# One stream of tokens in blocks of 256, 8 x 512 and 256 for the first part of a fused attention, convolution and Fourier kernel

## The chip, the core and the metric

The kernel runs on one core of a Trainium2 chip. TensorE (PE in the profile, with its weight loads as PEld) multiplies a moving tile by a stationary tile of 128x128 into PSUM, where the kernel keeps eight tiles of up to 512 fp32 columns (called banks here). VectorE (DVE) and ScalarE (ACT) do the elementwise work and read PSUM, GpSimd (POOL) does a few small copies, and SyncE (SP) issues the DMAs. The engines run their own lists of instructions in order and wait for each other through semaphores. The metric is the device time of one execution in microseconds (us). The kernel before takes 1354.01 us, the median of three runs (1353.06 to 1356.51).

## The reference

Three stages follow each other on 8 batches of 576 tokens and 512 features. All arithmetic is fp32.

```python
# 1. attention inside chunks of 64 tokens, 8 heads of 64 features
scores = scale * q_c @ k_c.T ; attn = softmax(scores) ; x = attn @ v_c      # x: 8 x 576 x 512
# 2. a gated layer with a 3-tap convolution over a batch's tokens
h = np.maximum(x @ w_in, 0.0)                                               # 512 -> 1024
conv_out = sum(conv_w[k] * hp[:, k:k + S, :] for k in range(3))             # hp: h with a zero token at both ends
x = h * sigmoid(conv_out) @ w_out                                           # 1024 -> 512
# 3. Fourier mixing over tokens and features, normalisation, and a wide layer
u = x + real(fft(fft(x, axis=1), axis=2)) ; un = (u - mu) / sqrt(var + 1e-6)
y = u + np.maximum(un @ w_ch1, 0.0) @ w_ch2                                 # 512 -> 2048 -> 512
```

## The kernel before

**Precision.** A product that has to be as good as fp32 is made of three fp32r matmuls: each operand is split into a high part (an fp32r copy, ACT) and a low part (the fp32 value minus the copy, DVE), and high x high, high x low and low x high are added in PSUM. Helper `split` (L279) records the two halves: `L280` is the ACT copy, `L281` the DVE subtraction.

**First part (about 0 to 600 us), the one that the change is about.** Tokens lie in the free dimension. Each batch is cut into 256 and 320 tokens (`NTOK`, L23), so there are 16 pieces, numbered i. For each piece:

- `attention(i, q)` (L364) does four heads at a time (q = 0, 1): scores (PE L386), maximum, exponential and normalisation (DVE L392 to L403, ACT L398), transposes of the attention (PE L411, ACT L414), values (PE L429 and L433), and the split of the result into tiles `x0..` (ACT L442, DVE L443). A piece of 320 tokens has five chunks, of which the fifth has instructions of its own. The `x0` tiles exist twice, once for pieces of either length.
- `m_step(i, f)` (L448), eight times: the product with one 128-wide slice of `w_in` (12 matmuls, PE L466), ReLU (ACT L486 or L496), the three taps (ACT L490 or L497, DVE L483 twice), the gate (ACT tanh L501, DVE L503), and the split into `gh` and `gl`. The last three tokens of h of the first piece of a batch are kept by POOL (L489) and put before those of the second piece (L495).
- `x_step(i, f)` (L514), eight times: the product of `gh`, `gl` with a slice of `w_out` into four PSUM banks, one per 128 features (12 matmuls, PE L534). After the eighth, ACT empties the four banks into `xlo` (tokens 0 to 287, with a mirrored copy of 32 tokens) and `xhi` (the other half in reverse), L550 to L572. The next piece's first x_step needs those banks empty.

Piece 0 uses plain fp32 matmuls (L457, L528) on weights that are still being turned from 64-bit words into fp32 (`to_float32`, DVE L293 to L297); only when a weight slice has been used there is it split.

After every second piece a batch is complete: `fold` (L577) adds and subtracts its halves, `d_step` (PE L642), `s_step` (PE L675) and `u_step` (PE L697) do the Fourier sums, and u goes to DRAM. `fold` makes `g` tiles on DVE, POOL repeats 33 columns of them twice (L594), and 355 columns are split. `fold_last` does that for the last batch in halves. `weight_sums` prepares `w_ch1` on DVE and PE-free time in between.

**Second part (about 610 us to the end).** `group` (PE L909) and `second` (PE L976) do the wide layer. Nothing in it is changed.

**What sets the order.** Every operation is recorded with an engine, an estimated cost, a priority `prio` and its dependencies. `Plan.emit` (L153) then writes one list per engine: at each step it takes the engine that can start first, and on it the ready operation with the least `prio`. Buffers are rings: `buf(pool, tag, n, ...)` waits for the n-th buffer before it. PSUM has two rings of four banks: tag `x` (the x_step's accumulators) and tag `o` (everything else). Priorities of the first part count in steps of one m_step; an x_step stands `lag` = 2.5 steps behind its m_step.

Of the kernel before, what the change touches and what calls it, by code (L numbers as in the profile page):

```python
# [8 lines left out]
F32 = mybir.dt.float32  # L9
# [9 lines left out]
B = 8  # L19
# [3 lines left out]
NTOK = (256, 320)  # L23
NOUT = (256, 322)
# [200 lines left out]
def kernel(  # L225
    ctx: ExitStack,
    tc: tile.TileContext,
    qk_a: bass.AP,
    qk_b: bass.AP,
    v_a: bass.AP,  # L230
    v_b: bass.AP,
# [15 lines left out]
    NH = 2 * B  # L247
# [66 lines left out]
    def load_dft(prio):  # L314
# [16 lines left out]
        h = buf("d", "fg", 2, [128, 640], F32R)  # L331
# [10 lines left out]
    early += [("d", tag, 1 + (tag == "fg")) for tag in ("f00", "f10", "f01", "f11", "fg")]  # L342
    early += [("s", "ds0", 1), ("s", "ds1", 1), ("s", "xlo", 2), ("s", "xhi", 1), ("d", "dd0", 1), ("d", "dd1", 1), ("d", "fw", 1)]
# [20 lines left out]
    def attention(i, q, prio):  # L364
        b, c = divmod(i, 2)
        n = NTOK[c] // 64
        hps = (2 * q, 2 * q + 1)
        qk, v = [], []
        for p, hp in enumerate(hps):
            qk.append(buf(*(("s", "xlo", 2) if (i, hp) == (0, HP - 1) else ("a", "qk", 3)), [128, 2, NTOK[c]]))  # L370
            load(qk[p], lambda hp=hp: (qk_a, qk_b)[c][b, hp], 1024 * NTOK[c], prio - 12 + p)
        for p, hp in enumerate(hps):
            v.append(buf("a", "v", 6, [128, NTOK[c]]))
            load(v[p], lambda hp=hp: (v_a, v_b)[c][b, hp], 512 * NTOK[c], prio - 10 + p)

        s = [buf("ps", "o" if i else "x", 4, [128, n, 64]) for _ in range(2)]
        low, high = slice(0, 64), slice(64, 128)
        half = (low, high)

        def qk_unit():  # L380
            todo = [(h, p, 2 * j + u, 2 * p + j, u) for j in range(2) for p in range(2) for u in range(2) for h in range(2)]
            if n == 5:
                todo += [(h, p, 4, 4, p) for p in range(2) for h in range(2)]
            for h, p, k, slot, u in todo:
                t, ks = qk[p](), slice(64 * k, 64 * k + 64)
                pe.matmul(s[h]()[half[u], slot, :], t[half[h], 0, ks], t[half[h], 1, ks], start=True, stop=True)  # L386
# [8 lines left out]
        for h in range(2):  # L395
            def exp(h=h):
                for k in range(n):
                    act.activation(out=es()[:, at_es(h, k), :], in_=s[h]()[:, k, :], func=ACT.Exp, scale=0.125, bias=mx()[:, h, k:k + 1], accum_out=sm()[:, at_es(h, k), :])  # L398

            op("ACT", 291 * n, exp, prio, r=[s[h], mx], w=[es, sm])  # L400
# [5 lines left out]
        tps = [buf("ps", "o", 4, [128, 4, 128])] + ([buf("ps", "o", 4, [128, 1, 128])] if n == 5 else [])  # L406

        def tr_unit():
            flat = es().rearrange("p a k -> p (a k)")
            for k in range(n):  # L410
                pe.transpose(tps[k // 4]()[:, k % 4, :], flat[:, 128 * k:128 * k + 128], ident)  # L411

        op("PE", 109 * n, tr_unit, prio + 2, r=[es], w=tps, spare=1)
        aop(512, lambda: act.copy(out=at()[:, 0:4, :], in_=tps[0]()), prio + 2, [tps[0]], [at], True)  # L414
        if n == 5:
            aop(128, lambda: act.copy(out=at()[:, 4:5, :], in_=tps[1]()), prio + 2, [tps[1]], [at], True)

        xp = [buf("ps", "o", 4, [128, 2, 2, 64]) for _ in range(2)] + ([buf("ps", "o", 4, [128, 2, 1, 64])] if n == 5 else [])
        hl = [buf("a", f"x0{k}{c}{q}", 1, [128, 2, n, 64], F32R if i else F32) for k in range(2 if i else 1)]
        for p, hp in enumerate(hps):  # L420
            x0[i, hp] = [Part(t, p) for t in hl]

        def pv_unit():
            for p in range(2):
                for u in range(2):
                    us = half[u]
                    for h in range(2):
                        for j in range(2):
                            pe.matmul(xp[j]()[half[h], p, u, :], v[p]()[half[j], 128 * u + 64 * h:128 * u + 64 * h + 64], at()[half[j], 2 * h + p, us], start=True, stop=True)  # L429
            if n == 5:  # L430
                for p in range(2):
                    for h in range(2):
                        pe.matmul(xp[2]()[half[h], p, 0, :], v[p]()[half[h], 256:320], at()[half[h], 4, half[p]], start=True, stop=True)  # L433

        op("PE", 210 + 142 * n, pv_unit, prio + 4, r=[*v, at], w=xp, after=[o for t in hl if t.before for o in t.before.readers])
        for j, x in enumerate(xp):
            part = lambda t, j=j: t()[:, :, 2 * j:min(2 * j + 2, n), :]
            k = 256 if j < 2 else 128
            if not i:
                aop(k, lambda x=x, part=part: act.copy(out=part(hl[0]), in_=x()), prio + 4, [x], [hl[0]], True)  # L440
                continue
            aop(k, lambda x=x, part=part: act.copy(out=part(hl[0]), in_=x()), prio + 4, [x], [hl[0]], True)  # L442
            vop(k, lambda x=x, part=part: dve.tensor_tensor(part(hl[1]), x(), part(hl[0]).bitcast(F32), op=ALU.subtract), prio + 4, [x, hl[0]], [hl[1]])  # L443
# [3 lines left out]

    def m_step(i, f, prio):  # L448
        c = i % 2
        n, no = NTOK[c], NOUT[c]  # L450
# [31 lines left out]
        def conv(k, lo, hi, src):  # L482
            vop(hi - lo, lambda: dve.scalar_tensor_tensor(cv()[:, lo:hi], in0=h()[:, src:src + hi - lo], scalar=tap(k), in1=cv()[:, lo:hi], op0=ALU.mult, op1=ALU.add), prio, [h, cw, cv], [cv], scalars=1)  # L483

        if c == 0:
            aop(256, lambda: act.activation(out=h()[:, :256], in_=acc(), func=ACT.Relu), prio, [acc], [h], True)  # L486
            hs[f] = buf("a", "hs", 9, [128, 3])
            keep = hs[f]
            op("POOL", 130, lambda: pool.tensor_copy(out=keep(), in_=h()[:, 253:256]), prio, r=[h], w=[keep])  # L489
            aop(256, lambda: act.activation(out=cv()[:, :256], in_=h()[:, :256], func=ACT.Copy, scale=tap(1)), prio, [h, cw], [cv], scalars=1)  # L490
            conv(0, 1, 256, 0)
            conv(2, 0, 255, 1)
        else:
            keep = hs[f]
            op("POOL", 130, lambda: pool.tensor_copy(out=h()[:, :3], in_=keep()), prio, r=[keep], w=[h])  # L495
            aop(320, lambda: act.activation(out=h()[:, 3:323], in_=acc(), func=ACT.Relu), prio, [acc], [h], True)  # L496
            aop(322, lambda: act.activation(out=cv()[:, :322], in_=h()[:, 1:323], func=ACT.Copy, scale=tap(1)), prio, [h, cw], [cv], scalars=1)  # L497
            conv(0, 0, 322, 0)
            conv(2, 0, 321, 2)
# [3 lines left out]
        vop(no, lambda: dve.scalar_tensor_tensor(to(), in0=cv()[:, :no], scalar=1.0, in1=h()[:, c:c + no], op0=ALU.add, op1=ALU.mult), prio, [cv, h], [cv if i else gh])  # L503
# [10 lines left out]
    def x_step(i, f, prio):  # L514
        b, c = divmod(i, 2)
        no = NOUT[c]
# [19 lines left out]
        if i < NH - 1 or f < FT - 4:  # L536
# [661 lines left out]
```

## Time and profile before

| | |
|---|---|
| median of three runs | 1354.01 us |
| profiled execution, its own time | 1353.37 us |
| its span (first to last instruction) | 1351.6 us |
| PE busy over the span | 1316.9 us (97%), 11040 matmuls |
| DVE, ACT, POOL busy | 1047.6 us (78%), 799.9 us (59%), 78.3 us (6%) |
| chain that ended last, by engine | PE 84%, DVE 9%, ACT 4% |
| mean granted TensorE clock | 0.994 of 2.4 GHz |

The 1.8 us between span and time lie outside the first and the last instruction. A matmul's busy time in a row is its latency, and matmuls overlap: the distance from one start to the next, or the length of a run of matmuls in the chain divided by their number, is what one costs in a stream. In the same way an ACT or DVE instruction's record overlaps the next one's.

### The profile page before, as it was taken

The page shows a single profiled execution, that of the slowest core. Times are in us where ns is not written, and L with a number is a line of the kernel's source. Part 1 is how long each engine was busy: PE and PEld are TensorE (multiplying, and loading weights), DVE is VectorE, ACT ScalarE, POOL GpSimd, SP SyncE. Part 2 cuts the span into 40 slices and gives each one's busy share as a digit, 9 for nine tenths or more (in the row PEclk, how much of TensorE's full clock was granted, in tenths as well). Part 3 has the DMA queues.
Part 4 walks back from the last instruction along what each step waited for, and adds up shares of the span by engine and source line. Part 5 has one row for each costly group of instructions (what it writes and reads, how often), then busy time and mean ns, then how long its engine had stood idle before and what let it go on. Part 6 is the DMA issues. An engine that isn't in the chain of part 4 may idle for free.

```text
span 1351.6 us, 28891 instructions
## 1 busy us (share of the span) xinstructions
PE 1316.9 (97%) x11040; PEld 1247.4 (92%) x11040; DVE 1047.6 (78%) x2028; ACT 799.9 (59%) x2132; POOL 78.3 (6%) x195
## 2 busy tenths in 40 slices
PE   5899999999999999998999999999999999999999
PEld 4799999999999999997999888888899999999998
DVE  7999888878987676867877858665498777777773
ACT  6777677867676776655765656566653333333331
POOL 1111020102010010210000000000000000000000
PEclk9999999999999999998999999999999999999999
DMA  8533525331632132136865766778755554554441
GB/s 309 151 93 116 169 66 178 99 121 53 191 110 80 53 117 73 51 107 201 251 206 173 222 199 182 231 218 264 212 157 177 161 172 140 158 172 134 164 141 40
DMA packets 154059, 206.46 MB, mean 153 GB/s; under 512 B 11072, under 2 KB 102848, under 8 KB 153920
## 3 DMA queue, kind: packets, MB, share of 16 engines
q1 hardware_dynamic: 153920, 204.61, 48.5%
q8 instruction: 87, 1.43, 0.4%
q14 instruction: 52, 0.43, 0.1%
HBM read 130.51 MB, written 74.06 MB: 151 GB/s over the span
## 4 chain that ended last, share of the span: by engine, by line
PE 84%; DVE 9%; ACT 4%; issue 1%; POOL 0%; DVEq 0%; ACTq 0%; POOLq 0%
PE x L909 22%; PE x L976 15%; PE o L976 12%; PE x L534 11%; PE o L466 11%; PE o L909 4%; PE o L642 2%; PE o L675 2%; ACT es L398 1%; DVE cv L483 1%; PE o L697 1%; PE o L808 1%; PE o L429 1%; PE o L386 1%; PE o L411 1%
## 5 line engine op out<-in xcount | busy, mean ns | idle before, releaser
L280 ACT CAST sxh<-raw 128x1024 fp32r<-128x1024 f32 (+1 forms) x143 | 146.0, 1029 | 193.5 <-PE o L976 84.2
L466 PE MATMUL o<-x,wih 128*128 128x320 f32 (+1 forms) x960 | 200.4, 302 | 2.6 <-DVE u L702 1.2
L281 DVE TENSOR_TENSOR sxl<-raw,sxh 128x1024 fp32r<-128x1024 f32 (+1 forms) x143 | 169.6, 1194 | 26.2 <-ACT sxh L280 26.1
L909 PE MATMUL x<-sxh,th 128*128 128x512 f32 (+1 forms) x480 | 177.5, 370 | 1.1 <-ACT sum L893 0.6
L909 PE MATMUL x<-sxh,tl 128*128 128x512 f32 (+1 forms) x480 | 176.4, 368 | 0.0
L909 PE MATMUL x<-sxl,th 128*128 128x512 f32 (+1 forms) x480 | 176.3, 367 | 0.0
L976 PE MATMUL x<-tl,sxh 128*128 128x256 f32 x576 | 163.0, 283 | 0.0
L976 PE MATMUL x<-th,sxl 128*128 128x256 f32 x576 | 163.0, 283 | 0.0
L976 PE MATMUL x<-th,sxh 128*128 128x256 f32 x576 | 163.0, 283 | 0.0
L466 PEld LDWEIGHTS o<-x,wih 128*128 128x128 f32 x960 | 153.0, 188 | 5.8 <-DVE x L443 2.0
L483 DVE SCALAR_TENSOR_TENSOR cv<-h,cw,cv 128x255 f32<-128x255 f32 (+2 forms) x256 | 128.9, 513 | 23.7 <-ACT cv L497 15.5
L534 PE MATMUL x<-gh,woh 128*128 128x322 f32 (+1 forms) x480 | 145.1, 302 | 0.0
L534 PE MATMUL x<-gl,woh 128*128 128x322 f32 (+1 forms) x480 | 142.5, 297 | 0.6 <-DVE gl L281 0.6
L534 PE MATMUL x<-gh,wol 128*128 128x322 f32 (+1 forms) x480 | 142.2, 296 | 0.0
L466 PE MATMUL o<-x,wil 128*128 128x320 f32 (+1 forms) x480 | 142.2, 296 | 0.1
L976 PE MATMUL o<-th,sxh 128*128 128x256 f32 x432 | 122.3, 283 | 0.0
L976 PE MATMUL o<-tl,sxh 128*128 128x256 f32 x432 | 122.3, 283 | 0.0
L976 PE MATMUL o<-th,sxl 128*128 128x256 f32 x432 | 122.3, 283 | 0.0
L976 PEld LDWEIGHTS x<-th,sxh 128*128 128x128 f32 x576 | 110.6, 192 | 0.2
L976 PEld LDWEIGHTS x<-tl,sxh 128*128 128x128 f32 x576 | 110.6, 192 | 0.0
L976 PEld LDWEIGHTS x<-th,sxl 128*128 128x128 f32 x576 | 110.6, 192 | 0.0
L885 DVE TENSOR_TENSOR u<-x,u 128x256 f32<-128x256 f32 (+2 forms) x112 | 55.8, 499 | 67.6 <-PE x L976 39.3
(287 smaller groups left out, 3166.8 us busy)
## 6 DMA issues: line engine op xcount, KB each, us to landing
raw<-h_scr SPq DMA_DIRECT2D x72, 512.0 KB, 5.2
h_scr<-sum SPq DMA_DIRECT2D x72, 256.0 KB, 3.1
u<-u_scr SPq DMA_DIRECT2D x66, 256.0 KB, 3.3
qk<-in_qk_b SPq DMA_DIRECT2D x32, 320.0 KB, 3.4
h_scr<-sum SPq DMA_DIRECT2D x48, 192.0 KB, 2.7
out_y<-u SPq DMA_DIRECT2D x35, 256.0 KB, 2.5
wide<-in_w_ch SPq DMA_DIRECT2D x16, 512.0 KB, 4.9
u_scr<-u SPq DMA_DIRECT2D x32, 256.0 KB, 2.6
```

Of the source, the lines that this page charges most:

```text
L280: aop(n, lambda: act.copy(out=cut(h()), in_=cut(src())), prio, [src], [h], psum, after=after)
L281: vop(n, lambda: dve.tensor_tensor(cut(l()), cut(src()), cut(h()).bitcast(F32), op=ALU.subtract), prio, [src, h], [l])
L386: pe.matmul(s[h]()[half[u], slot, :], t[half[h], 0, ks], t[half[h], 1, ks], start=True, stop=True)
L398: act.activation(out=es()[:, at_es(h, k), :], in_=s[h]()[:, k, :], func=ACT.Exp, scale=0.125, bias=mx()[:, h, k:k + 1], accum_out=sm()[:, ...
L466: pe.matmul(acc(), w[:, ws], x, start=k == 0, stop=k == 11)
L483: vop(hi - lo, lambda: dve.scalar_tensor_tensor(cv()[:, lo:hi], in0=h()[:, src:src + hi - lo], scalar=tap(k), in1=cv()[:, lo:hi], op0=ALU. ...
L534: pe.matmul(accs[d](), w[:, dsl], x, start=f == 0 and k == 0, stop=f == FT - 1 and k == 2)
L642: pe.matmul(acc()[:rows, :], x, w, start=k == 0 and n == 0, stop=k == 1 and n == 2)
L675: pe.matmul(accs[sine]()[:rows, :], w, x, start=n == 0, stop=n == len(todo) - 1)
L885: vop(n, lambda: dve.tensor_tensor(cut(x()), acc(), cut(x()), op=ALU.add), prio, [acc, x], [x])
L909: pe.matmul(acc(), a, b, start=first and m == 0, stop=m == 5, skip_group_check=not first)
L976: pe.matmul(acc(), a, b, start=first and m == 0 and gs[0] == 0, stop=gs[-1] == FG - 1 and m == len(todo) - 1, skip_group_check=not first)
```

## The change

The 4608 tokens of all batches become one stream that is cut into ten blocks, whatever the batches' borders: 256, eight times 512, 256. The number of matmuls with 256 to 322 moving columns is replaced by fewer with 512. Along with this:

- attention works on one or two windows of 256 tokens (`nw`), its last part (`values`, with the split) is recorded separately and waits until the block before has done its last m_step, since the `x0` tiles now exist once;
- the three tokens of h are carried from each block to the next; a block's outputs end two tokens before its inputs, and a tap that would cross a batch's border is left out by cutting the DVE instruction in two there;
- `spread` empties the banks for the one or two batches that a block holds;
- fewer buffers: `h` 2 (3), `cv` 2 (4), `gh` and `gl` 3 (4), `qk` 2 (3), `v` 4 (6), `es`, `mx`, `sm` 1 (2); `xhi` 2 (1);
- `fold` writes its sums over `v`, splits 289 columns, and POOL repeats the columns in both halves of the split (`repeat`), eight copies instead of four;
- `s_step` has no `q` tile; `lag` is 3.2, and priorities count 36 tokens as one step.

A batch is complete with the block that holds its last token: batches 0, 1, 2 with blocks 1, 2, 3, batch 3 with block 5 (two of its tokens lie there), batches 4 to 7 with blocks 6 to 9.

```diff
-NTOK = (256, 320)
-NOUT = (256, 322)
+SIZE = (256,) + 8 * (512,) + (256,)
+NBLK = len(SIZE)
+AT = tuple(sum(SIZE[:i]) for i in range(NBLK + 1))
+OUT = (0,) + tuple(a - 2 for a in AT[1:-1]) + AT[-1:]
...
+    def attention(i, q, prio, last):
+        nw = SIZE[i] // 256
+        n = 4 * nw
...
+        def qk_unit():
+            for w in range(nw):
+                for j in range(2):
+                    for p in range(2):
+                        for u in range(2):
+                            for h in range(2):
...
+        op("PE", 310 + 470 * nw, qk_unit, prio, r=qks, w=s)
+        es, mx, sm = buf("a", "es", 1, [128, 2 * n, 64]), buf("a", "mx", 1, [128, 2, n]), buf("a", "sm", 1, [128, 2 * n, 1])
...
+        return lambda: values(i, q, nw, v, at, last)
...
+    def values(i, q, nw, v, at, last):
...
+        op("PE", 310 + 470 * nw, pv_unit, last, r=[*v, at], w=xp, after=m_done[i - 1] if i > 1 else ())
...
+            aop(256 * nw, lambda part=part, src=src: act.copy(out=part(hl[0]), in_=src()), last, [x], [hl[0]], True)
+            if i:
+                vop(256 * nw, lambda part=part, src=src: dve.tensor_tensor(part(hl[1]), src(), part(hl[0]).bitcast(F32), op=ALU.subtract), last, [x, hl[0]], [hl[1]])
...
     def m_step(i, f, prio):
-        c = i % 2
-        n, no = NTOK[c], NOUT[c]
+        n, no = SIZE[i], OUT[i + 1] - OUT[i]
...
-        h, cv = buf("a", "h", 3, [128, 323]), buf("a", "cv", 4, [128, 322])
-        gh, gl = buf("a", "gh", 4, [128, no], F32R if i else F32), buf("a", "gl", 4, [128, no], F32R) if i else None
+        m_done[i] = [done]
+        h, cv = buf("a", "h", 2, [128, 515]), buf("a", "cv", 2, [128, 512])
+        gh, gl = buf("a", "gh", 3, [128, no], F32R if i else F32), buf("a", "gl", 3, [128, no], F32R) if i else None
...
+        for k in (0, 2):
+            skip = [t - OUT[i] for t in range(0 if k == 0 else 575, AT[-1], 576) if OUT[i] <= t < OUT[i + 1]]
+            edges = [-1, *skip, no]
+            for lo, hi in zip(edges, edges[1:]):
+                conv(k, lo + 1, hi)
...
     def x_step(i, f, prio):
...
+        for b in range(B):
+            t0, t1 = max(OUT[i] - 576 * b, 0), min(OUT[i + 1] - 576 * b, 576)
+            if t0 < t1:
+                spread(b, t0, t1, 576 * b - OUT[i], accs, prio, end)
...
+            put(hi, lambda x, y, d=d: back(hi_at(b, d), 575, x, y), max(t0, 288), t1, d, p, end and d >= 2)
+            put(lo, lambda x, y, d=d, lo=lo: lo()[:, d, x - 1:y - 1], max(t0, 1), min(t1, 288), d, p)
+            put(lo, lambda x, y, d=d, lo=lo: lo()[:, d, 287:288], t0, min(t1, 1), d, p)
+            put(lo, lambda x, y, d=d, lo=lo: back(lo()[:, d], 607, x, y), max(t0, 288), min(t1, 320), d, p)
...
+    def repeat(x, prio, ks=slice(0, 2)):
+        for r in (NFOLD, NFOLD + 33):
+            op("POOL", 130, lambda r=r: pool.tensor_copy(out=x()[:, ks, r:r + 33], in_=x()[:, ks, 256:NFOLD].bitcast(F32)), prio, r=[x], w=[x])
...
-            split(*hl, g, 2 * NREP, prio + sine, cut=lambda t: t[:, :, :NREP])
+            aop(578, lambda g=g, h=h: act.copy(out=h()[:, :, :NFOLD], in_=g()), prio + sine, [v], [h])
+            vop(578, lambda g=g, h=h, l=l: dve.tensor_tensor(l()[:, :, :NFOLD], g(), h()[:, :, :NFOLD].bitcast(F32), op=ALU.subtract), prio + sine, [v, h], [l])
+            for x in hl:
+                repeat(x, prio + sine)
...
-    lag = 2.5
+    lag = 3.2
+    place = lambda i, f: AT[i] / 36 + f * SIZE[i] / 288
...
+            rest = [attention(i + 1, q, *((t + (u - t) * (0.05 + 0.4 * q), u - 1.5 + 0.3 * q) if i else (t - 3.5 + 3 * q, t + 0.5 + 3 * q))) for q in range(2)]
```

The lists that the planner writes move at two places that matter below. The first is PE at the end of piece (block) 0. L457 (L459 after) is an m_step of block 0, L528 (L531) one of its x_steps, L386 (L393) are scores, L466 (L468) are m_steps of the next block; the last name of a row of block 0 is where its weight slice is kept. Before:

```order
L528 MATMUL x<-gh,ds_596 128x256 x4
L386 MATMUL o<-qk 64x64 x16
L528 MATMUL x<-gh,xlo 128x256 x4
L457 MATMUL o<-x_348,dd_808 128x256 x2
L457 MATMUL o<-x_362,dd_808 128x256 x2
L466 MATMUL o<-x_662,wih 128x320
L466 MATMUL o<-x_669,wih 128x320
L466 MATMUL o<-x_662,wil 128x320
```

After:

```order
L418 MATMUL o<-ident,es 128x128 x4
L459 MATMUL o<-gl,dd_820 128x256 x4
L531 MATMUL x<-gh,dd_810 128x254 x4
L435 MATMUL o<-at,v 64x64 x32
L393 MATMUL o<-qk 64x64 x32
L531 MATMUL x<-gh,fw 128x254 x4
L468 MATMUL o<-x_720,wih 128x512
L468 MATMUL o<-x_726,wih 128x512
L468 MATMUL o<-x_720,wil 128x512
```

The first m_step of block 1 stood right behind the last m_step of block 0, ahead of its last two x_steps (`dd_816` and `fw`, further down); it now stands behind all of them.

The second place is DVE where a batch has just been completed (batch 2) and the next block begins. L581 (L602) is the first instruction of `fold`, which reads `xlo` and `xhi`; L483 (L488) are the taps, L503 (L507) the gate, L392 (L398) the maximum of the scores. Before:

```order
L483 SCALAR_TENSOR_TENSOR cv<-h,cw,cv 128x255 x4
L503 SCALAR_TENSOR_TENSOR cv<-cv,h 128x256
L581 TENSOR_TENSOR fw<-xlo,xhi 128x2x287
L503 SCALAR_TENSOR_TENSOR cv<-cv,h 128x256
L581 TENSOR_TENSOR fw<-xlo,xhi 128x2x287
L281 TENSOR_TENSOR gl<-cv,gh 128x256 x2
L584 TENSOR_TENSOR fz<-fw 128x4x128
L483 SCALAR_TENSOR_TENSOR cv<-h,cw,cv 128x255
```

After:

```order
L726 TENSOR_TENSOR u<-t,o 64x512
L602 TENSOR_TENSOR fw<-xlo,xhi 128x2x287 x2
L488 SCALAR_TENSOR_TENSOR cv<-h,cw,cv 128x450
L398 TENSOR_REDUCE mx<-o 128x8
L488 SCALAR_TENSOR_TENSOR cv<-h,cw,cv 128x61
L398 TENSOR_REDUCE mx<-o 128x8
L488 SCALAR_TENSOR_TENSOR cv<-h,cw,cv 128x449
L399 TENSOR_SCALAR mx<-mx 128x16
L605 TENSOR_TENSOR fz<-fw 128x4x128
L488 SCALAR_TENSOR_TENSOR cv<-h,cw,cv 128x62
L605 TENSOR_TENSOR fz<-fw 128x4x128
```

Before, two m_steps of the next piece had their taps done when fold came; now both halves of fold stand ahead of the first taps, and these come in four pieces, with a batch's border between them.

## Rows read from the trace of the kernel before

**Rows 1.** Windows: us; busy us (instructions) of PE, PEld, DVE, ACT, POOL; clock; DMA.

```profile
100.00:300.00 200.00, 197.24 (x2184) 190.51 (x2184) 174.37 (x418) 145.38 (x536) 25.86 (x67) 1.00 0.38 122
300.00:596.00 296.00, 293.99 (x3044) 286.28 (x3041) 227.53 (x551) 206.60 (x738) 34.52 (x93) 1.00 0.30 96
```

**Rows 2.** Chain that ended last, 310 to 330: start, us, engine, tile, line, matmuls.

```profile
309.95 1.42 PE o L466 x12
311.37 1.77 PE x L534 x12
313.14 0.74 PE o L386 x40
313.88 1.97 PE x L534 x12
```

**Rows 3.** The same chain, 565 to 590: twelve matmuls of 320 columns.

```profile
567.68 1.76 PE o L466 x12
```

**Rows 4.** The same chain, 800 to 840: thirty matmuls of 512 columns.

```profile
819.31 6.80 PE x L909 x30
```

**Rows 5.** Timeline of PE, 53 to 72: start, length, line, tiles, shapes.

```profile
59.72 0.65 PE L466 MATMUL o<-x,wih 128*128 128x320 f32 x2
...
61.76 0.69 PE L386 MATMUL o<-qk 64*64 64x64 f32 x32
62.38 1.99 PE L528 MATMUL x<-gh,dd 128*128 128x256 f32 x8
64.22 0.60 PE L411 MATMUL o<-ident,es 128*128 128x128 f32 x4
64.57 0.54 PE L466 MATMUL o<-x,wih 128*128 128x320 f32 x2
```

**Rows 6.** Timeline of PE, 247 to 254: values, border of two pieces.

```profile
247.65 0.69 PE L429 MATMUL o<-at,v 64*64 64x64 f32 x32
248.16 0.41 PE L433 MATMUL o<-at,v 64*64 64x64 f32 x8
248.50 0.51 PE L466 MATMUL o<-x,wih 128*128 128x256 f32 x2
...
252.88 0.28 PE L534 MATMUL x<-gh,woh 128*128 128x256 f32 x1
```

**Rows 7.** Timeline of ACT, 247 to 258: the banks are emptied between pieces.

```profile
247.82 0.40 ACT L566 ACTIVATE xhi<-x 128x288 f32<-128x288 f32 x1
248.13 0.19 ACT L567 ACTIVATE xlo<-x 128x34 f32<-128x34 f32 x1
248.21 0.41 ACT L566 ACTIVATE xhi<-x 128x288 f32<-128x288 f32 x1
...
251.88 0.39 ACT L572 ACTIVATE xhi<-x 1x287 f32<-1x287 f32 x1
```

**Rows 8.** Timeline of DVE, 60 to 67: the last steps of piece 0.

```profile
59.95 0.68 DVE L281 TENSOR_TENSOR wil<-u,wih 128x512 fp32r<-128x512 f32 x1
60.55 0.68 DVE L281 TENSOR_TENSOR wil<-f,wih 128x512 fp32r<-128x512 f32 x1
...
65.49 0.41 DVE L503 SCALAR_TENSOR_TENSOR gh<-cv,h 128x256 f32<-128x256 f32 x1
65.83 0.41 DVE L392 TENSOR_REDUCE mx<-o 128x4 f32<-128x256 f32 x1
```

**Rows 9.** Waits, 80 to 610: engine, line, waited for; us in total, times, longest.

```profile
DVE cv L483 <- ACT cv L497: 15.5, 12, 3.4
```

**Rows 10.** Timeline of PE, 596 to 640: the end of the first part.

```profile
596.41 2.80 PE L675 MATMUL o<-ab,ds 128*128 128x258 f32 x22
601.39 1.23 PE L642 MATMUL x<-dd,f 128*128 128x258 f32 x3 [2.18 <-ACT f L280]
...
610.43 0.44 PE L909 MATMUL x<-sxh,th 128*128 128x384 f32 x1 [0.25 <-DVE ab L281]
```

**Rows 11.** Timeline of POOL, 596 to 632: the repeated columns of the last batch.

```profile
600.93 3.28 POOL L623 COPY fg<-fg 128x33 f32<-128x33 f32 x8 [3.55 <-DVE fg L620]
```

More of the change, by code (lines that the diff above doesn't have):

```diff
@@ L362, with heads @@
     x0 = {}
[L364 to L374, printed above, removed]
+    def heads(i):
+        shape = [128, 2, SIZE[i] // 64, 64]
+        for q in range(2):
+            hl = [buf("a", f"x0{k}{q}", 1, shape, F32R) for k in range(2)] if i else [buf("a", "gl", 3, shape)]
+            for p in range(2):
+                x0[i, 2 * q + p] = [Part(t, p) for t in hl]
@@ new lines, in attention @@
+    def attention(i, q, prio, last):
+        nw = SIZE[i] // 256
+        n = 4 * nw
+        blk = AT[i] // 256
+        half = (slice(0, 64), slice(64, 128))
+        qks, v = [], []
+        for p in range(2):
+            qks.append(buf(*(("s", "xlo", 2) if i + q == 1 and not i else ("a", "qk", 2)), [128, nw, 2, 256]))
+            load(qks[p], lambda p=p: qk[blk:blk + nw, 2 * q + p].rearrange("w r a t -> r w a t"), 262144 * nw, prio - 12 + p)
+        for p in range(2):
+            v.append(buf("a", "v", 4, [128, nw, 256]))
+            load(v[p], lambda p=p: v_in[blk:blk + nw, 2 * q + p].rearrange("w r t -> r w t"), 131072 * nw, prio - 10 + p)
@@ L405, in attention @@
         at = buf("a", "at", 2, [128, n, 128])
[L406 to L414, printed above, removed]
@@ L435, in attention, with tr_unit @@
-        op("PE", 210 + 142 * n, pv_unit, prio + 4, r=[*v, at], w=xp, after=[o for t in hl if t.before for o in t.before.readers])
-        for j, x in enumerate(xp):
[L437 to L443, printed above, removed]
+        for c in range(nw):
+            tps = buf("ps", "o", 4, [128, 4, 128])
+            def tr_unit(c=c, tps=tps):
+                flat = es().rearrange("p a k -> p (a k)")
+                for k in range(4):
+                    pe.transpose(tps()[:, k, :], flat[:, 512 * c + 128 * k:512 * c + 128 * k + 128], ident)
+            op("PE", 436, tr_unit, prio + 2, r=[es], w=[tps], spare=1)
+            aop(512, lambda c=c, tps=tps: act.copy(out=at()[:, 4 * c:4 * c + 4, :], in_=tps()), prio + 2, [tps], [at], True)
@@ L480, in m_step @@
         tap = lambda k: cw()[:, 3 * f + k:3 * f + k + 1]
[L482 to L493, printed above, removed]
+        off = 3 + OUT[i] - AT[i]
@@ new lines, in spread @@
+        back = lambda t, first, lo, hi: t[:, first - hi + 1:first - lo + 1][:, ::-1]
+        for d in (0, 2, 1, 3) if end else range(DT):
+            p, lo, hi = prio + (end and d % 2), los[d % 2], his[d % 2]
+            put(hi, lambda x, y, d=d: back(hi_at(b, d), 575, x, y), max(t0, 288), t1, d, p, end and d >= 2)
+            put(lo, lambda x, y, d=d, lo=lo: lo()[:, d, x - 1:y - 1], max(t0, 1), min(t1, 288), d, p)
+            put(lo, lambda x, y, d=d, lo=lo: lo()[:, d, 287:288], t0, min(t1, 1), d, p)
+            put(lo, lambda x, y, d=d, lo=lo: back(lo()[:, d], 607, x, y), max(t0, 288), min(t1, 320), d, p)
@@ L1040 @@
                     s_step(b, m, t + 5 + m if b == B - 1 else t + 6 + 2 * m)
-    end = NH * FT + lag
+    assert not later and not norms and first
+    end = 16 * FT + lag
     def turn(old, new, side, prio):
```

207 lines of the change are left out of this document (103 added, 104 removed).

## The prediction

> **What bounds the kernel now.** I read the windows first, then the chain, then single stretches of the timelines. Between 100 and 596 us, where the first part runs steadily, PE is busy for all but 4.8 us at full clock, DVE for 87% of the time up to 300 us and 77% after it, ACT for about 70% [rows 1]. The chain there is PE beside PE, m_steps and x_steps with short attention units between them [rows 2], so the first part lasts as long as its PE instructions take, and one matmul's price in a stream decides. That price is a run's length by its number: 118.3 ns for 256 columns, 147.5 for 322 [rows 2], 146.7 for 320 [rows 3]. The second part has runs of 512 columns: 226.7 ns [rows 4]. A matmul of 512 thus costs 1.92 times one of 256, and about 10 ns do not depend on columns. Two stretches are bound otherwise. Up to about 70 us PE waits for weights that DVE converts: DVE instructions stand without a gap, one of 512 columns every 0.60 us [rows 8]. And from 596.4 to 610.4 us the last batch runs down a chain of ACT, DVE and PE [rows 10].
>
> **The stream, -14.1 us.** Pieces 1 to 15 are eight of 320 and seven of 256, each with 96 matmuls in m_steps and 96 in x_steps. By the prices above: 768 x 146.7 + 768 x 147.5 + 1344 x 118.3 ns = 385.0 us. Blocks 1 to 8 have 8 x 192 x 226.7 ns = 348.2 us and block 9 192 x 118.3 = 22.7 us: 370.9 us. All of it lies on the path, in the stretch where PE hardly waits. The low end is the line through 256 and 512 alone: 1152 fewer matmuls x 9.9 ns and 1344 fewer columns give 12.0 us; I take the rows as they are.
>
> A rule speaks against most of this term. The Trainium skill, page "TensorE: Matmul & The Clock Gate", section "Back-to-back issue gap", gives a matmul its columns at 2.4 GHz and some 2.5 ns beside. By it 1152 fewer matmuls would be worth 3.4 us with the columns, and the sum would end some 10.7 us higher. The trace disagrees at every length it has (118.3, 146.7, 226.7 ns), and the rows go into the sum.
>
> **Attention, -11 us.** It has as many matmuls as before, in fewer units. Five chunks cost 0.74 us for the scores [rows 2], 0.85 for the values (247.65 to 248.50) [rows 6] and some 0.44 for five transposes (four take 0.35) [rows 5]; four chunks cost 0.62 for scores (61.76 to 62.38) [rows 5], 0.51 for values [rows 6] and 0.35. With 16 and 14 such units behind piece 0 that is 16 x 2.03 + 14 x 1.48 = 53.2 us. Eight further records cost 0.12 us, so eight chunks take 1.10 + 0.99 + 0.70 = 2.79 us: 16 x 2.79 + 2 x 1.48 = 47.6 us, 5.6 less. Besides, an x_step behind such a unit takes 1.97 instead of 1.77 us [rows 2]: 0.20 us for every unit that stands alone. Scores, values and transposes make 90 units before and, by the order after, about 63 groups: 27 x 0.20 = 5.4 us. The bounds are -5.6 (no edge is saved) and -12.
>
> **The start, +4.3 us.** Before, the first m_step of piece 1 starts at 59.7 us, and the last two x_steps of piece 0 run between m_steps of piece 1, the first of them at 62.4 [rows 5]. After, all of block 0 comes first, so block 1 waits for the last gate of block 0. On DVE that gate ends at 65.9 us [rows 8]. The list up to it has three more weight splits (3 x 0.60 us) and attention for 512 tokens instead of 320 and 256 (some 0.8 us): 68.5 us. The last x_step follows (1.84 us, 62.38 to 64.22), and block 1 starts at about 70.8 us, 11.1 later. Of these, 6.8 us are PE work done ahead: two x_steps (3.7), longer scores, transposes and values of block 1 (2 x 0.76) and the scores of block 2 (2 x 1.10 against 0.62). What is left, 4.3 us, PE stands idle. Bounds: 0 (the splits done early would have been waited for later) and twice the value.
>
> **The borders, +4 us.** This is what the trace before can't show: blocks of 512 with the `x0` tiles there once, two `h` and two `cv`. Behind a block's last x_step PE has u_step transposes (0.46 us), scores (1.30), five m_steps (13.6) and transposes (0.46): 15.8 us until the new block's first x_step. In that time ACT empties the banks: 22 instructions for a block with one border. Before, 14 of them and 11 others took from 247.8 to 252.3 us, with 0.30 us for 288 columns and 0.08 for 34 [rows 7]; 20 of the 22 and a ReLU are 3.6 us, after which fold may start. Behind it DVE has, up to the first `gl`, fold's two sums (1.3), four cut taps (1.4), two maxima (1.2), a weight conversion (1.5), gate (0.6), the normalisation (1.4) and fold's further entries and the split (2.5): about 10 us. With the hops some 14.3 us pass against 15.8 of cover, so the first x_step is just in time. Before, the same turn cost PE nothing: from 248.50 to 252.88 us it ran three m_steps without a gap [rows 6]. I take half a microsecond for each of the eight borders. The upper end is the longest wait of a tap for ACT in this stretch, 3.4 us [rows 9], eight times: 27 us. The low end is nothing. The wait of `values` for the last m_step has cover: two x_steps, s_step and u_step stand between the values and the new m_step, over 7 us for two ACT copies and two subtractions of 0.60 us each per half.
>
> **The end, +0.5 us.** The last block leaves 258 columns and 2 mirrored ones, not 288, 34 and 32: some 0.5 us less on ACT. The Fourier matmuls of batch 6 that now stand behind the last x_step (about 2.5 us more than before) fall into the gap before 601.39, where PE waited 2.2 us [rows 10]. Against this, POOL repeats twice as often, 16 instead of 8 copies of 0.41 us [rows 11], and the first weight splits of the second part wait for the last copy: +3.3 us at most. Bounds -3 and +3.5. Extra DVE instructions where a tap is cut (112 pieces, each with 0.09 us of its own by the difference of 0.60 for 512 and 0.34 for 256 columns [rows 8]) cost 10 us of DVE; 192 fewer taps, gates and splits give back 17. I cost both at nothing: DVE has 94 us free between 100 and 596 [rows 1]. If that cover were gone, the first rival below holds.
>
> **Sum.** -14.1 - 11.0 + 4.3 + 4.0 + 0.5 = -16.3 us on 1353.4 us (the profiled execution, 1.8 us of it outside the span): 1337.1, and 0.6 more against the median of the runs: 1337.7 us.
>
> **Rivals.** *DVE becomes the bound up to 300 us.* It is busy 87% there [rows 1]; PE's work shrinks by some 4%, DVE's hardly. What speaks against it is that DVE stays near 91%. If it took the whole gain of that stretch (200 of some 530 us, 9 of 25 us), the change would be worth 7 us: 1347. Chance 0.13.
>
> *Nothing stalls.* The borders cost nothing, the early splits come back as time later, the end is 1.5 us shorter: -14.1 - 11 - 1.5 + 1 = -25.6, 1328. For it: the same turn was free before. Against it: 1.5 us of slack on 16. Chance 0.22.
>
> *The borders drain.* One mechanism: fold stands ahead of the new block's first taps on DVE and waits for ACT's emptying, so `gl` is late, the four banks of tag `o` fill with m_steps, and PE stops. At 3.4 us per border [rows 9] this is 27 instead of 4: +6.9, 1361. It turns the change slower from (16.3 + 4) / 8 = 2.5 us per border on. Against it: PE's list runs five m_steps ahead there. Chance 0.09.
>
> *A matmul costs by its columns.* If the 512 columns of an m_step or x_step cost twice those of 256, the stream saves 1344 columns, 0.6 us, and the sum is -2.8: 1351. The rows 4 are from other lines with other tiles, but of the same shape and type. The rule weighed above would give some 3 us more. Chance 0.03.
>
> *The second part does not start earlier* because something else than the last batch sets it. Its matmuls follow the last Fourier ones closely [rows 10]. Then about 1354. Chance 0.03.
>
> **How the numbers follow.** The forecast keeps 0.50, with a range of its own of 1331 to 1344 us (attention and start at their bounds). For 8 times in 10 I take 1325 to 1352: it leaves out the drained borders and the rare best case. A run can tell about 0.3% (4 us) from no change: faster than that are the forecast, the second rival and most of the first, 0.85; within it the last two and a remainder, 0.06; slower the drained borders, 0.09.
>
> **What would show it.** Runs of 24 to 60 matmuls of L468 and L537 at 227 ns each prove the stream; single scores units of about 1.1 us with 1.3 us to the next unit prove attention. The first L468 should start near 71 us, the last x_step end near 577 to 581 and the first L933 follow 14 us later. PE idle between 100 us and there should be under 10 us; idle before L537 where a block begins, released by DVE's `gl`, means the borders drain. Runs of 240 ns, or a DVE without gaps up to 300 us, would show where the forecast is wrong.

## The result, and the profile after

The changed kernel takes 1337.47 us (median of four runs, 1335.39 to 1340.18) against 1354.09 us; the ratio is 0.9876, with a 95% interval of 0.9852 to 0.9899. That is 16.6 us less; the forecast was 16.3 less. The sum is right, but its largest term is not: it was almost 10 us too large, and other terms made up for that. The profiled execution took 1338.54 us, with a span of 1336.8 us.

The windows of the changed kernel over the steady stretch answer to [rows 1] (busy us of PE, PEld, DVE, ACT, POOL with instructions, clock, DMA share, GB/s):

```profile
100.00:300.00 200.00, 197.88 (x1705) 165.16 (x1704) 165.34 (x331) 137.90 (x474) 38.74 (x85) 1.00 0.36 119
300.00:581.00 281.00, 279.15 (x2428) 236.34 (x2428) 213.62 (x458) 183.32 (x600) 48.16 (x120) 1.00 0.31 98
```

PE is idle for 4.0 us here, 4.8 before: the borders of the blocks cost no more than those of the pieces did. DVE has become less busy (83% and 76%, from 87% and 77%), so it did not turn into the bound by its share alone.

The chain that ended last, 300 to 345 us, answers to [rows 2, 3] (start, us, engine, tile, line, matmuls):

```profile
312.10 2.80 PE o L468 x12
...
316.43 11.40 PE o L468 x48
...
328.27 2.78 PE x L537 x12
...
338.17 2.98 PE x L537 x12
```

and the same chain in the second part, whose code is unchanged, to [rows 4]:

```profile
804.40 6.80 PE x L933 x30
```

Here is the first surprise. A matmul of 512 columns costs 232 to 238 ns in the stream (11.40 us / 48, 2.78 / 12) and still 226.7 in the second part. A run here is a row of neighbouring matmuls of one line. Over the distances between neighbouring starts inside the runs from 100 to 575 us (some 640 for either line; the 52 above 300 ns, all of them a run's first or second, are left out), the means are 233.6 ns for m_steps and 232.0 for x_steps.

PE at the start answers to [rows 5] (start, length, line, tiles, shapes; in brackets the wait before it):

```profile
62.66 1.88 PE L531 MATMUL x<-gh,dd 128*128 128x254 f32 x8
64.46 1.16 PE L435 MATMUL o<-at,v 64*64 64x64 f32 x64
66.80 0.33 PE L393 MATMUL o<-qk 64*64 64x64 f32 x2 [1.18 <-ACT es L404]
68.42 1.16 PE L393 MATMUL o<-qk 64*64 64x64 f32 x62 [1.30 <-DVE x L444]
69.51 3.50 PE L531 MATMUL x<-gh,fw 128*128 128x254 f32 x8
72.45 1.17 PE L468 MATMUL o<-x,wih 128*128 128x512 f32 x2
```

The first m_step of block 1 starts at 72.45 us (forecast: 70.8). After the two waits the last x_step of block 0 takes 2.94 us (69.51 to 72.45), where one with the same shape took 1.80 at 62.66: the granted clock of 60 to 75 us is 0.89 (line further down), a part of it at 1.2 GHz.

The end answers to [rows 10]:

```profile
582.27 2.51 PE L699 MATMUL o<-ab,ds 128*128 128x258 f32 x16
...
586.71 0.74 PE L721 MATMUL o<-ident,xhi 128*128 128x128 f32 x4 [1.45 <-ACT t L708]
588.17 2.92 PE L699 MATMUL o<-ab,ds 128*64 128x258 f32 x14 [0.71 <-DVE u L726]
590.88 0.85 PE L666 MATMUL x<-dd,f 128*128 128x258 f32 x3
...
597.83 0.33 PE L933 MATMUL x<-sxh,th 128*128 128x384 f32 x1
```

The last x_step ends at 581.5 us, just past the 577 to 581 of the forecast, and the first L933 follows 16.3 us later (forecast: 14).

**The ledger.** I added up, by line, the distances from each PE instruction's start to the next, and the waits in them apart, for both profiled executions. From the first matmul to the last it is 1344.4 us before and 1329.5 after, 14.9 less:

| PE's time, us | before | after | difference |
|---|---|---|---|
| m_steps and x_steps behind block 0, without waits | 399.6 | 388.0 | -11.6 |
| attention, without waits | 63.7 | 58.9 | -4.8 |
| block 0, without waits | 32.2 | 33.3 | +1.1 |
| Fourier, without waits | 95.5 | 94.0 | -1.5 |
| all waits up to 100 us | 15.2 | 19.4 | +4.2 |
| all waits, 100 to 570 us | 4.8 | 4.0 | -0.8 |
| all waits, 570 to 620 us | 6.6 | 5.2 | -1.4 |

The rest (weight sums, the second part) differs by less than 0.4 us. In the first row, 385.1 us before and 380.6 after are the matmuls at their prices inside a run. What lies above that is 12.9 us in the 114 runs that have an attention unit at one end before, 5.8 us in 61 such runs after, and 1.5 us in all other runs, before as after.

### The profile page after: what moved, and what is told of

Read it like the earlier page. It is cut to its first block, busy times and chain, and to the rows that moved or that the text cites. A ratio compares the mean times of both kernels' runs of the same rounds, so it can differ in the third digit from the quotient of the medians.

```text
span 1336.8 us, 26161 instructions
## 1 busy us (share of the span) xinstructions
PE 1300.0 (97%) x9888; PEld 1164.6 (87%) x9888; DVE 1025.7 (77%) x1832; ACT 765.7 (57%) x1902; POOL 109.5 (8%) x247
## 4 chain that ended last, share of the span: by engine, by line
PE 89%; DVE 6%; ACT 2%; issue 1%; DMA 0%; SPq 0%; ACTq 0%; DVEq 0%
PE x L933 22%; PE x L1000 16%; PE o L468 14%; PE x L537 13%; PE o L1000 12%; PE o L933 4%; PE o L666 3%; PE o L699 2%; PE o L832 1%; PE o L721 1%; PE o L393 1%; DVE cv L488 1%; PE o L418 1%; PE o L435 1%; ACT th L279 0%
## 5 line engine op out<-in xcount | busy, mean ns | idle before, releaser
L933 PE MATMUL x<-sxh,th 128*128 128x512 f32 (+1 forms) x480 | 177.5, 370 | 0.8 <-ACT sum L917 0.6
L468 PE MATMUL o<-x,wih 128*128 128x512 f32 (+1 forms) x576 | 175.8, 388 | 1.8 <-ACT at L421 0.7
L933 PE MATMUL x<-sxh,tl 128*128 128x512 f32 (+1 forms) x480 | 176.6, 368 | 0.0
L933 PE MATMUL x<-sxl,th 128*128 128x512 f32 (+1 forms) x480 | 176.5, 368 | 0.0
L488 DVE SCALAR_TENSOR_TENSOR cv<-h,cw,cv 128x1 f32<-128x1 f32 (+30 forms) x272 | 129.0, 494 | 25.9 <-ACT cv L498 25.2
L468 PEld LDWEIGHTS o<-x,wih 128*128 128x128 f32 x576 | 104.1, 189 | 24.0 <-ACT h L493 1.5
L537 PE MATMUL x<-gh,woh 128*128 128x512 f32 (+1 forms) x288 | 112.6, 391 | 0.0
L537 PE MATMUL x<-gh,wol 128*128 128x512 f32 (+1 forms) x288 | 110.3, 383 | 0.0
L468 PE MATMUL o<-x,wil 128*128 128x512 f32 (+1 forms) x288 | 110.0, 382 | 0.0
L537 PE MATMUL x<-gl,woh 128*128 128x512 f32 (+1 forms) x288 | 109.6, 381 | 0.2
```

The lines of the kernel that those rows point to most:

```text
L468: pe.matmul(acc(), w[:, ws], x, start=k == 0, stop=k == 11)
L537: pe.matmul(accs[d](), w[:, dsl], x, start=f == 0 and k == 0, stop=f == FT - 1 and k == 2)
L933: pe.matmul(acc(), a, b, start=first and m == 0, stop=m == 5, skip_group_check=not first)
```

## The experiments

All times are medians, with the ratio to the kernel before (run beside it) and its interval. The changed kernel itself was run again as the measure for the rest.

> The changed kernel unchanged, as the measure for the runs beside it: 1337.5 us, 0.9876 of before within 0.3%. Matmuls of 512 columns inside a run at 233.6 ns (m_step) and 231.9 ns (x_step), 227 ns in the second part.

Measured: 1337.86 us, ratio 0.9878 (0.9862 to 0.9895), matmuls at 233.6 and 232.0 ns.

### What a matmul of 512 columns costs in place

```diff
-                    pe.matmul(acc(), w[:, ws], x, start=k == 0, stop=k == 11)
+            for c in range(0, n, 256):       # the twelve products on columns c to c+255, then the next half
+                        pe.matmul(acc()[:, c:c + 256], w[:, ws], x[:, c:c + 256], ...)
```

> Each m_step of a 512-token block is done in two halves of 256 columns, first half complete, then the second: 768 matmuls of 512 become 1536 of 256, x_steps as they are. The prediction's rows (226.7 for 512, 118.3 for 256) give 768 x 9.9 ns = +7.6 us; the prices measured in the changed kernel (233.6 and 119.5) 768 x 5.4 ns = +4.1 us; 'a matmul costs by its columns' +0.3 us. Expected: 1341.5 us, 0.3% over the changed kernel.

Measured: 1343.84 us, ratio 0.9922 (0.9904 to 0.9939), 6.0 us over the changed kernel. Its chain (L469 is the m_step here):

```profile
314.26 2.87 PE o L469 x24
...
318.66 11.71 PE o L469 x96
...
330.81 2.78 PE x L537 x12
```

A half costs 119.6 to 122 ns, and m_steps take 4.6 us more of PE's time in all, 198.4 for 193.8. That is near the 4.1 of the prices in place and well under the 7.6 of [rows 4]. So fewer, wider matmuls do save time here, but only some 6 ns for each, not 10, with the tiles where they stand.

### Where the tiles stand in SBUF

What else differs between L933 and L468? Not the load beside them: matmuls under a busy DVE, ACT or POOL had the same mean as the others, within 1 ns. But the single distances repeat from one run to the next (correlation 0.73 for L468 and 0.92 for L537 over some 700 matmuls each), which speaks for something fixed in the program. So I moved tiles, with every engine's list unchanged; where a tile starts is read off the compiled program.

```diff
-            hs[f] = buf("a", "hs", 9, [128, 3])
+            hs[f] = buf("a", "hs", 10, [128, 3])     # one 32-byte tile more: cv, gh, x0 move by 32 bytes
```

> One more 32-byte tile of tag hs, so that cv, gh and the x0 tiles start at a multiple of 64 bytes in SBUF instead of 32 past one; every engine's list of instructions stays the same. Theory 'alignment' (a moving tile of 512 columns that starts 32 bytes past a multiple of 64 costs some 5 to 6 ns more): m_step matmuls fall from 233.6 to 227 ns, x_step matmuls with gh from 233.6 to 227 to 229 ns, together 768 x 6.6 + 512 x 5 + 256 x 1.5 ns = 8 us of PE work, about 7 us of time: 1330.5. Rival 'what the tiles are for' (the stream's price is one of its own operands, its busy neighbours DVE and ACT, or its place high in SBUF): prices and time unchanged, 1337.5 within 1.5 us.

Measured: 1335.58 us, ratio 0.986 (0.9845 to 0.9875). m_steps fell to 232.2 ns, x_steps to 230.0. The correlation with the unmoved kernel, instruction by instruction, is gone for L468 (below 0.05), while L933, whose tiles were not moved, stays at 227.1 ns.

```diff
-    cw = buf("a", "cw", 1, [128, FT * 3])
+    cw = buf("a", "cw", 1, [128, FT * 3 + 8])        # at, gl and everything behind move by 32 bytes
```

> cw is made 32 bytes longer instead, which moves everything behind it: at, gl and one of two h then start 32 bytes past a multiple of 64, and cv, gh and x0 at a multiple. Every list stays the same. Alignment: m_steps at 227 ns as with the extra hs tile, x_step matmuls with gl rise from 229 to about 233.6 and those with gh fall to 227 to 229; 1 to 2 us slower than with the extra hs tile, 1332. What the tiles are for: gl stays at 229 and gh and m_steps at 233.6, 1337.5.

Measured: 1337.7 us, ratio 0.9877 (0.9863 to 0.9892): m_steps 232.3, x_steps 231.7 ns; the matmuls with gl rose from 229.3 to 231.4. So addresses do set the price, but alignment to 64 bytes is not the rule: m_steps got back 1.3 of 6.6 ns.

```diff
-    pools["w"] = tc.alloc_tile_pool(name="wts", bufs=1)
     pools["a"] = tc.alloc_tile_pool(name="heads", bufs=1)
+    pools["w"] = tc.alloc_tile_pool(name="wts", bufs=1)      # and 10 hs tiles
```

> As with the extra hs tile (all moving tiles at a multiple of 64 bytes), and the attention pool lies below the weights in SBUF, so moving tiles stand at 31 to 84 kB and weights at 76 to 142 kB, much as in the second part; every list stays the same. If the 232 ns in the stream against 227 in the second part are due to where the two operands stand relative to each other, prices fall to 227 to 229 and the time to 1331. If they are due to what the stream does beside (its banks, its neighbours), they stay at 232 and 230 and the time at 1335.5.

Measured: 1334.6 us, ratio 0.9865 (0.985 to 0.988). m_steps fell to 228.1 ns; x_steps stayed at 231.2, now with gl as the dear one (233.0) and gh cheaper (230.0). Here x0, gh and the weights all start at a multiple of 512 bytes, and gl 128 bytes past one. In all five places, L933 among them, the cheap matmuls were those whose weight and moving tile stand at the same place modulo 256 bytes (for three in four of L933's matmuls the weight stands 256 bytes further modulo 512, and they cost the same 227 ns). That was a pattern found afterwards, so it had to forecast something:

```diff
-            hs[f] = buf("a", "hs", 9, [128, 3])
+            hs[f] = buf("a", "hs", 14, [128, 3])     # gh and x0 at 128 bytes modulo 512, like weights and gl
```

> Tag hs gets 14 tiles instead of 9 (160 bytes more), so that gh and the x0 tiles start 128 bytes past a multiple of 512 like the weights and gl; every list stays the same. From the four traces so far: a matmul of 512 columns costs 227 to 229 ns where the next weight and the moving tile start at the same place modulo 256 bytes (as in all of the second part), 231 to 234 where they don't. By that, m_steps fall from 233.6 to 227.5 to 228 and x_steps from 232 to 228.5 ns: 768 x 5.8 + 768 x 3.5 = 7.1 us: 1330.5. Rival, absolute alignment to 64 bytes alone: as with one more hs tile, 1335.5 (232 and 230.4 ns). Rival, a chance of addresses: anything between.

Measured: 1332.31 us, ratio 0.984 (0.9826 to 0.9854), some 5 us under the changed kernel. Its chain:

```profile
308.30 2.72 PE o L468 x12
...
312.55 11.11 PE o L468 x48
...
324.10 2.77 PE x L537 x12
```

| start modulo 256: weights / x0 / gh / gl | m_step, ns | x_step, ns |
|---|---|---|
| changed kernel: 128 / 224 / 224 / 128 | 233.6 | 232.0 |
| one hs tile more: 128 / 0 / 0 / 128 | 232.2 | 230.0 |
| cw longer: 128 / 0 / 0 / 160 | 232.3 | 231.7 |
| pools swapped: 0 / 0 / 0 / 128 | 228.1 | 231.2 |
| 14 hs tiles: 128 / 128 / 128 / 128 | 227.8 | 228.5 |
| second part (L933), all 128 | 227.1 (this line) | |

The m_step's 227.5 to 228 and the x_step's 228.5 came as forecast; the time stayed 1.8 us above its forecast (m_steps and x_steps take 6.1 us less of PE's time, not 7.1). What in the chip makes the phase count stays open. The kernel before had the difference already, at 322 columns: its four gl tiles start at 128, 160, 192 and 224 modulo 256, its weights at 128, and the matmuls with the first cost 145.8 ns, with the others 147.1, 149.5 and 149.1. For 256 columns no such difference shows: 119.9 ns in the changed kernel, 119.7 with 14 hs tiles.

### Half of the sizes undone

```diff
-SIZE = (256,) + 8 * (512,) + (256,)
+SIZE = (256,) + 4 * (512,) + 9 * (256,)
```

> Blocks of 256, four times 512 and nine times 256: half of the change of size is undone. By the prices measured in the changed kernel (232.9 and 119.3 ns) 768 matmuls of 512 that become 1536 of 256 cost 768 x 5.7 = 4.4 us, eight double attention units that become sixteen 8 x 0.17 = 1.4 us, and some 90 more unit borders at 0.05 us on average 4.5 us: +10, 1347.5 us. By the prediction's prices 768 x 9.9 = 7.6, 1.4 and 24 x 0.2 = 4.8 us: +13.8, 1351.5. If the gain came from the dropped pieces of 320 and not from 512: no change.

Measured: 1352.37 us, ratio 0.9993 (0.9984 to 1.0003), near the prediction's terms and above the trace's prices. Its profiled execution (1349.61 us, the fastest of ten) has 11.7 us more span than the changed kernel run again: m_steps and x_steps 7.1 us (4.4 by the prices inside runs, 2.7 beside attention), attention's own matmuls 4.4 us; what else moved cancels out. So blocks of 512, not the mere end of the pieces of 320, carry the gain, and the wider matmuls alone are the smaller part of it.

### Attention in smaller units

```diff
-        op("PE", 310 + 470 * nw, qk_unit, prio, r=qks, w=s)
+        for w in range(nw):                              # and the values likewise
+            op("PE", 780, lambda w=w: qk_unit(w), prio + w, r=qks, w=s)
```

> Scores and values of a 512-token block are recorded as one PE operation per window of 256 again, so that m_steps and x_steps can come between: 10 more runs of scores and 2 more of values in PE's list. The prediction's attention term (0.08 us per further split of a unit, 0.2 us for the unit that stands alone) gives +12 x 0.2 = 2.4 us: 1340. If an edge costs nothing in the stream: 1337.5 within 1 us.

Measured: 1342.06 us, ratio 0.9921 (0.9904 to 0.9938), some 5 us over the changed kernel (3.8 in the profiled span). In its trace the scores come in two units with other work between:

```profile
312.24 0.69 PE L392 MATMUL o<-qk 64*64 64x64 f32 x30 [0.33 <-ACT t L705]
...
315.76 0.60 PE L721 MATMUL o<-ident,xlo 128*64 128x128 f32 x4
316.29 0.69 PE L392 MATMUL o<-qk 64*64 64x64 f32 x32
```

where the changed kernel has one:

```profile
315.27 1.16 PE L393 MATMUL o<-qk 64*64 64x64 f32 x64
```

m_steps and x_steps take 2.8 us more of PE's time, scores 1.3 more. A unit that stands alone thus costs about what the prediction took for it (12 x 0.2 us); the planner's other moves lie in the figure too.

### How much cover a border has

In the trace of the changed kernel I had measured how long each block's first `gl` was ready before PE read it (0.6 to 7.2 us), and took that for the border's cover.

```diff
-            vop(574, lambda d=d: dve.tensor_tensor(v()[:, d:d + 2, 0:287], ..., op=ALU.add), prio, [lo, hi], [v])
+            vop(574, lambda d=d: [dve.tensor_tensor(v()[:, d:d + 2, 0:287], ..., op=ALU.add) for _ in range(3)][-1], ...)
```

> Each of fold's first two sums is done three times instead of once (28 more DVE instructions of 0.65 us, 2.6 us at each of seven borders, 18 us in all); the lists are otherwise the same. In the trace of the changed kernel the first gl of a block is ready 2.4, 0.6, 2.8, 3.5, 7.2, 2.9, 1.7 us before PE wants it at these borders; by that cover the extra 2.6 us cost 0.2 + 2.0 + 0.9 = 3 us: 1340.5. By the prediction's cover of 1.5 us everywhere 7 x 1.1 = 7.7 us: 1345. If DVE is what bounds the first part, all 18 us: 1355.

Measured: 1360.13 us, ratio 1.0054 (1.0039 to 1.0069): 22 us for some 19 us of DVE work. My reading of the cover was wrong. What PE waits for, 75 to 590 us (us in total, times, longest):

```profile
PE o L468 <- DVE x L444: 4.2, 2, 2.4
PE x L537 <- DVE gl L280: 3.5, 7, 0.8
PE o L468 <- ACT h L493: 2.1, 2, 1.8
PE o L418 <- DVE es L409: 2.1, 2, 1.5
```

against this in the changed kernel:

```profile
PE o L435 <- DVE x L444: 1.3, 1, 1.3
...
PE o L468 <- DVE x L444: 0.5, 2, 0.3
```

The reason stands in DVE's timeline of the changed kernel at a border. L444 makes the low half of `x0`; the first m_step needs the last of the four:

```profile
246.16 0.69 DVE L444 TENSOR_TENSOR x<-o,x 128x512 fp32r<-128x512 f32 x1 [0.39 <-ACT x L442]
246.76 0.75 DVE L602 TENSOR_TENSOR fw<-xlo,xhi 128x574 f32<-128x574 f32 x1
247.43 0.68 DVE L444 TENSOR_TENSOR x<-o,x 128x512 fp32r<-128x512 f32 x1
248.03 0.75 DVE L602 TENSOR_TENSOR fw<-xlo,xhi 128x574 f32<-128x574 f32 x1
...
249.42 0.68 DVE L444 TENSOR_TENSOR x<-o,x 128x512 fp32r<-128x512 f32 x1
```

The sums of fold (L602) stand between the subtractions, and the m_step starts after a wait for the last one:

```profile
250.16 0.73 PE L468 MATMUL o<-x,wih 128*128 128x512 f32 x2 [0.35 <-DVE x L444]
```

Each us put there reaches PE. The waits of PE between 72 us and the end of the stream are some 13 us longer than in the changed kernel; the clock falls after them (0.97 granted from 200 to 300 us, 0.98 from 500 to 600), which makes matmuls longer too.

The control puts as much work into the middle of a block:

```diff
+            reps = 5 if f == 4 and i in (2, 3, 4, 6, 7, 8, 9) else 1      # the subtraction that makes gl
```

> 28 more DVE instructions again (the subtraction that makes gl is done five times instead of once), 0.6 us each, 17 us in all, 2.4 us in each of seven blocks, but in the middle of the block (f = 4), not where fold stands; no instruction is moved. If the 22 us that the tripled sums of fold cost are the border's (its chain has no cover left), most of this is hidden: the first x_step matmul with this gl had 2.2, 5.5, 9.4, 0.1, 3.8, 2.0 and 1.8 us to spare, which leaves some 3 to 5 us: 1342. If DVE bounds the whole first part, 17 to 20 us: 1356.

Measured: 1349.79 us, ratio 0.997 (0.996 to 0.9981): 12 us for 17 us of work. PE's longest wait there:

```profile
PE x L540 <- DVE gl L512: 4.4, 4, 2.8
```

So 70% shows in the middle and all of it at the border. A DVE that is busy for 80% of the time has, in this kernel, little to spare at these places: of its some 95 us of waits from 100 to 575 us in the changed kernel, 42 are for ACT before taps, gate and `gl`, inside the chain of an m_step, and 22 for ACT's exponentials. Both expectations by slack fell; the rival that DVE bounds the stretch came nearer.

### The x_step's distance, undone

```diff
-    lag = 3.2
+    lag = 2.5
```

> lag is 2.5 again instead of 3.2: x_steps stand 0.7 steps (of 36 tokens each, that is not a full m_step) nearer to their m_steps. In PE's list the m_steps ahead of a block's first x_step become 4, 3, 6, 4, 5, 4, 5, 4, 5 instead of 5, 4, 5, 5, 5, 4, 5, 4, 6. If the m_steps ahead are what covers the border, the three borders that lose one (2.8 us) inside the stream stall by what the spare 2.9, 2.4 and 2.8 us don't cover, and those after follow: 1 to 4 us slower, 1340. If a border's cover doesn't matter: 1337.5 within 1 us.

Measured: 1330.49 us, ratio 0.9822 (0.9809 to 0.9835): 7.4 us faster than the changed kernel, not slower. At the start one x_step of block 0 stands behind the first m_step of block 1 again:

```profile
66.59 1.15 PE L393 MATMUL o<-qk 64*64 64x64 f32 x62 [1.10 <-ACT es L404]
68.24 0.73 PE L468 MATMUL o<-x,wih 128*128 128x512 f32 x2 [0.49 <-DVE x L444]
...
71.14 1.87 PE L531 MATMUL x<-gh,fw 128*128 128x254 f32 x8
```

The windows from 60 to 75 and from 580 to 620 us, of the changed kernel:

```profile
60.00:75.00 15.00, 12.53 (x169) 10.32 (x168) 15.00 (x30) 11.60 (x52) 3.02 (x3) 0.89 0.44 157
...
580.00:620.00 40.00, 34.66 (x224) 32.46 (x223) 32.12 (x64) 21.25 (x53) 4.58 (x16) 0.91 0.43 130
```

and with lag 2.5:

```profile
60.00:75.00 15.00, 12.99 (x175) 10.50 (x174) 15.00 (x30) 12.17 (x52) 3.37 (x4) 1.00 0.51 175
...
580.00:620.00 40.00, 35.57 (x226) 33.14 (x226) 33.55 (x64) 24.72 (x51) 5.66 (x16) 1.00 0.62 192
```

By the ledger 3.3 us are shorter waits of PE, and 4.3 us shorter instructions, most of them in block 0 and the Fourier sums, beside the stretches where the changed kernel had the low clock. The mean clock was 0.999 to 1.000 in all four runs, 0.993 to 0.997 in those of the changed kernel.

### Both together

> lag 2.5 and 14 hs tiles together; the lists are those of the kernel with lag 2.5, only the addresses differ. If the two gains are independent (lag 2.5: start, clock and a few stalls, 7.4 us; phase of the moving tiles: 5.5 us of matmul time, 768 x 5.8 + 768 x 2.7 ns = 6.5 by the prices), 1337.9 - 7.4 - 5.5 = 1325. If shorter matmuls only uncover DVE, which the tripled sums of fold and the five-fold subtraction have shown to have little to spare, part of it turns into waits: 1328.

Measured: 1325.91 us (1325.21 to 1326.29), ratio 0.9797 (0.9783 to 0.981), 11 to 12 us under the changed kernel and the fastest of all. m_steps cost 227.9 ns, x_steps 228.3; the gains add up to within 1 us. The windows of its profiled execution:

```profile
60.00:75.00 15.00, 13.00 (x168) 10.43 (x167) 13.88 (x28) 11.25 (x49) 3.04 (x4) 0.89 0.53 176
...
580.00:620.00 40.00, 37.38 (x230) 35.79 (x229) 32.66 (x62) 26.80 (x52) 1.82 (x13) 0.96 0.69 211
```

The lists are those of lag 2.5, and yet the clock was low again at both places. Against 14 hs tiles alone its profiled execution gains 6.6 us from PE's first matmul to its last, 5.5 of them shorter waits. So the waits are the part of lag 2.5's gain that both runs show; how much of it the clock is stays open.

## Why the prediction came out right

- **What bounds it: right.** PE beside PE, from 72 us to the end of the stream, with 4 us of waits.
- **The stream, -14.1 us: the step that was mis-sized.** "I take the rows as they are" took the 226.7 ns of another line, with the same shape and type but tiles that stand otherwise in SBUF. Inside runs it is now 768 x 233.6 + 768 x 232.0 + 192 x 120.1 ns = 380.6 us, against 768 x 146.4 + 768 x 148.0 + 1344 x 118.3 = 385.1 before: -4.5. With the prices of the kernel with 14 hs tiles, 227.8 and 228.5 ns, it would be -11.6, and that kernel did get some 6 us of PE's time back. The Trainium skill, page "TensorE: Matmul & The Clock Gate", section "Back-to-back issue gap", gives some 2.5 ns beside the columns for a matmul by itself, and for a stream of weight loads and matmuls some 131 ns at 512 columns, which the prediction left out. Neither holds here: with the phase right, 227.8 ns is 14.5 more than 512 columns at 2.4 GHz.
- **Attention, -11.0: right.** Its own matmuls gave -4.8 (5.6 forecast). The edges lie in the m_steps and x_steps beside it: from 12.9 to 5.8 us, -7.1 (5.4 forecast).
- **The start, +4.3: right in size, not whole.** PE waits 4.2 us more up to 100 us. Block 0's PE work grew by 1.1 us besides, at the lower clock, which no term held. That all of block 0 stands ahead was taken as given; it is the work of lag 3.2, as the run with 2.5 shows.
- **The borders, +4.0: zero, and for another reason than thought.** Waits from 100 to 570 us went from 4.8 to 4.0. But the chain named, ACT's emptying to fold to `gl`, is not the tightest: the subtractions for `x0`, behind fold's sums on DVE, are. PE's m_steps wait for them already (0.5 us in two waits), and its x_steps show no wait for `gl`. The rival "the borders drain" was near: 2.7 us more of DVE work at each of seven borders made the kernel slower than before.
- **The end, +0.5: -2.9.** Waits from 570 to 620 us are 1.4 us shorter and the Fourier instructions, of the whole first part, 1.5.
- **DVE cuts at nothing: right for this kernel** (PE waits no longer), but the cover named, 94 free us, is not cover: 17 us of it cost 12 where they were put.

So 9.6 us of stream that didn't come, and 1.1 in block 0, were balanced by borders (4.8) and end (3.4) that cost less than allowed for, and by 0.9 more from attention. Right by its sum, by its bound and by attention; lucky in that errors both ways were of like size.

## What to carry to other kernels

Take a matmul's price from a run with the same operands in the same place, and where none exists keep both ends in the range. Judge an in-order engine's cover by adding work at the very place, not by its share of busy time or by one consumer's slack; and ask of each wait which of its inputs stands behind other work in the list. When a tuned constant is changed along with a structure, undo it alone: here that gave almost half as much as the whole change.

## What the runs showed of the hardware

- In these kernels a matmul of 512 columns costs 227 to 230 ns where its weights and moving tile start at the same place modulo 256 bytes in SBUF, and 231 to 234 ns where they do not. Single distances repeat from run to run (correlation 0.73 and 0.92). Padding of 160 bytes was worth 5 us of 1338.
- Waits of 1.2 and 1.3 us with 62 small matmuls behind them were followed by the low clock: the eight matmuls of an x_step took 2.94 us instead of 1.80. Another order of the same work had neither this nor the low stretch at the end in one profiled execution, and its instructions were 4.3 us shorter; with the tiles moved as well, the same order had both again.
